# One hardware loop for the TensorE program of a decode attention kernel, with loads of 32 KB per partition

## The chip, the cores and the metric

The kernel runs on one core of one Trainium2 chip. The metric is the device time of one execution in microseconds (us), as the median of several executions. The profiled execution gives a "span", from its first to its last instruction, which is about 2 us shorter than its time.

PE is TensorE's matmul stream, PEld its weight loads, DVE VectorE, ACT ScalarE, SP the engine that issues the loads. All loads run on the core's 16 DMA engines. A "packet" is one record of one DMA engine: here one row of a load, or, as an "instruction packet", a piece of an engine's own program that is fetched. "Share" is the busy share of the 16 DMA engines together.

## The reference

Two decode attentions with one query position each, concatenated:

```python
# A: 32 heads, each with its own cache of 32768 keys;  Dh = 128, D = 512
q = (x @ wq).reshape(1, 1, 32, 128).transpose(0, 2, 1, 3)
scores = einsum("bhqd,bhkd->bhqk", q, k_cache) * 128 ** -0.5
o = einsum("bhqk,bhkd->bhqd", softmax(scores), v_cache)
a = o.transpose(0, 2, 1, 3).reshape(1, 1, 4096) @ wo
# B: the same with 32 query heads on 8 caches, and only the last 4096 keys of each
return concatenate([a, b], axis=-1)            # (1, 1, 1024), bf16
```

A's caches are 2 x 32 x 32768 x 128 bf16 numbers, 537 MB; everything together is 570 MB, and each byte is used once. In the kernel before, the load queue fills 98.5% of the 16 DMA engines' span (q1 below), so the least time is taken here as the time of the loads.

## The kernel before

Keys are loaded with a run of consecutive keys on each partition, transposed on PE in tiles of 128x128, copied from PSUM to SBUF by DVE, multiplied by the query (S), and the probabilities are transposed back (PT) and multiplied by V (PV). PE works in "rounds": 8 heads by 8192 keys for A. Helpers record every operation with what it depends on; the waits are then written out, so each engine's program is one straight line.

```python
a["KC"], b["KC"] = 4, 2            # A: a round is 2048*4 = 8192 keys by 32/4 = 8 heads
NK, NV, NT = 4, 3, 3               # 4 K slots of 2 MB, 3 V slots of 4 MB, 3 PSUM banks for transposes

def kv_src(self, name, which, h0, nh, r):      # one head: 64 keys = 16 KB per partition
    ap = d[which][0, h0:h0 + nh, base:base + d["blk"], :]
    return ap.rearrange("s (p j) d -> p s (j d)", p=128)

def emit_PV(self, i, u):           # 64 matmuls of 256 columns for 4 MB of V
    for kc in range(KC):
        for jj in range(4):
            for c in range(STRIPS):
                inst = e.matmul(acc[32*c:32*c+HG, 0:w], lhsT=pt[:, col:col+HG],
                                rhs=vv[:, :, 16*kc + 4*c + jj, :], ..., tile_position=(0, 32*c))
# ... end of the program: V of the last round, B's weights in between, A's weights last
for u in range(d["nvu"]):
    self.load_v(last, u, 0); self.load_v(last, u, 1)
    if u in (1, 2): self.load_wo("B", u - 1)
    if u == d["nvu"] - 1:
        for part in range(3): self.load_wo("A", part)
        self.emit_proj("B", ...)
    self.emit_PV(last, u)
self.emit_proj("A", ...)
```

## Time and profile before

| | before |
|---|---|
| time, median of 3 | 1368.06 us |
| span of the profiled run | 1365.0 us |
| first data packet, from the start | 2.06 us |
| last data packet | 1357.5 us, 7.6 us before the end |
| PE / DVE busy | 70% / 56% |
| instruction packets of PE | 119 of 16 KB |

The lines below are from the page of the kernel before. The strings of digits and the GB/s are 40 equal slices of the span; the queue lines give packets, MB and the share of 16 engines' span; then comes the chain of waits by engine, and the last line is the group of PE's transposes (busy us, mean ns of one, then idle time before them and what ended most of it).

```profile
span 1365.0 us, 32343 instructions
...
PE 951.6 (70%) x15172; PEld 734.7 (54%) x15172; DVE 767.8 (56%) x1414; ACT 29.9 (2%) x73; POOL 2.4 (0%) x11
...
DMA  9999999999999999999999999999999999999995
GB/s 392 422 425 426 427 426 427 427 425 427 425 426 427 426 426 427 425 426 427 427 424 427 425 427 427 425 426 426 427 426 425 426 426 428 426 426 425 426 405 213
...
q1 hardware_dynamic: 40340, 570.44, 98.5%
q8 instruction: 119, 1.95, 0.6%
...
DMA 77%; PE 20%; DVE 1%; issue 1%; SPq 0%; ACT 0%
...
L417 PE MATMUL psT<-ident,kbuf 128*128 128x128 bf16 x8448 | 641.3, 243 | 361.2 <-DMA kbuf<-in_A_k_cache_dram 294.9
```

DMA is busy in every slice but the last, it is 77% of the chain of waits, and PE's transposes idle 295 us for K. The rate stands at 426 GB/s for 36 slices. The end by stretches (columns: stretch, its length, busy us of each engine, PE clock, DMA share, GB/s):

```profile
...
600.00:1290.00 690.00, 485.77 (x7866) 379.57 (x7864) 395.20 (x699) 12.69 (x32) 0.00 (x0) 0.85 1.01 426
...
1300.00:1304.00 4.00, 3.70 (x97) 2.63 (x94) 2.77 (x6) 0.00 (x0) 0.00 (x0) 1.00 0.60 250
1304.00:1338.00 34.00, 11.87 (x203) 7.08 (x203) 6.58 (x28) 1.74 (x5) 0.00 (x0) 0.70 1.00 423
1340.00:1356.00 16.00, 9.59 (x96) 4.54 (x95) 2.26 (x6) 0.00 (x0) 0.00 (x0) 0.71 0.52 218
```

### The profile page before, as it was taken

The page shows a single profiled execution, that of the slowest core. Times are in us where ns is not written, and L with a number is a line of the kernel's source. Part 1 is how long each engine was busy: PE and PEld are TensorE (multiplying, and loading weights), DVE is VectorE, ACT ScalarE, POOL GpSimd, SP SyncE. Part 2 cuts the span into 40 slices and gives each one's busy share as a digit, 9 for nine tenths or more (in the row PEclk, how much of TensorE's full clock was granted, in tenths as well). Part 3 has the DMA queues.
Part 4 walks back from the last instruction along what each step waited for, and adds up shares of the span by engine and source line. Part 5 has one row for each costly group of instructions (what it writes and reads, how often), then busy time and mean ns, then how long its engine had stood idle before and what let it go on. Part 6 is the DMA issues. An engine that isn't in the chain of part 4 may idle for free.

```text
span 1365.0 us, 32343 instructions
## 1 busy us (share of the span) xinstructions
PE 951.6 (70%) x15172; PEld 734.7 (54%) x15172; DVE 767.8 (56%) x1414; ACT 29.9 (2%) x73; POOL 2.4 (0%) x11
## 2 busy tenths in 40 slices
PE   5689766776777687676667767766766767687646
PEld 4466555655555465555556545555655545465423
DVE  4688555655656555564655646555565656555431
ACT  0000000000000000000000000000000000000000
POOL 0000000000000000000000000000000000000000
PEclk9889878878988887887888888878888898887877
DMA  9999999999999999999999999999999999999995
GB/s 392 422 425 426 427 426 427 427 425 427 425 426 427 426 426 427 425 426 427 427 424 427 425 427 427 425 426 426 427 426 425 426 426 428 426 426 425 426 405 213
DMA packets 40762, 572.51 MB, mean 419 GB/s; under 512 B 4659, under 2 KB 4661, under 8 KB 4789
## 3 DMA queue, kind: packets, MB, share of 16 engines
q1 hardware_dynamic: 40340, 570.44, 98.5%
q8 instruction: 119, 1.95, 0.6%
q14 instruction: 15, 0.11, 0.0%
q10 hardware_dynamic: 288, 0.00, 0.0%
HBM read 570.43 MB, written 0.00 MB: 418 GB/s over the span
## 4 chain that ended last, share of the span: by engine, by line
DMA 77%; PE 20%; DVE 1%; issue 1%; SPq 0%; ACT 0%
DMA kbuf<-in_A_k_cache_dram 73%; PE psT L417 15%; PE psS L444 3%; DMA kbuf<-in_B_k_cache_dram 3%; DMA vbuf<-in_A_v_cache_dram 2%; PE psS L583 1%; PE psACC L525 1%; DVE kt L421 0%; SPq L203 0%; DVE oc_B L551 0%; PE psPT L565 0%; ACT psb L472 0%; DVE o_B L535 0%; DVE tr_in L460 0%; DVE nbg_B L491 0%
## 5 line engine op out<-in xcount | busy, mean ns | idle before, releaser
L421 DVE COPY kt<-psT 128x1024 bf16<-128x1024 bf16 x1056 | 672.5, 685 | 427.0 <-PE psT L417 423.7
L417 PE MATMUL psT<-ident,kbuf 128*128 128x128 bf16 x8448 | 641.3, 243 | 361.2 <-DMA kbuf<-in_A_k_cache_dram 294.9
L417 PEld LDWEIGHTS psT<-ident,kbuf 128*128 128x128 bf16 x8448 | 577.5, 111 | 489.8 <-DMA kbuf<-in_A_k_cache_dram 335.6
L444 PE MATMUL psS<-kt,qz_A 128*32 128x512 bf16 x2048 | 177.2, 427 | 0.0
L525 PE MATMUL psACC<-vbuf,ptsb 128*8 128x256 bf16 (+1 forms) x4160 | 132.9, 283 | 23.9 <-issue 21.7
L525 PEld LDWEIGHTS psACC<-vbuf,ptsb 128*8 128x8 bf16 (+1 forms) x4160 | 103.0, 89 | 55.2 <-issue 23.4
L537 DVE SCALAR_TENSOR_TENSOR o_A<-o_A,alpha_A,psACC 128x256 f32<-128x256 f32 x48 | 23.1, 480 | 87.5 <-PE psACC L525 87.5
L444 PEld LDWEIGHTS psS<-kt,qz_A 128*32 128x32 bf16 x2048 | 32.1, 97 | 31.5 <-issue 10.4
L472 ACT ACTIVATE psb<-psS,nb_A 128x512 bf16<-128x512 f32 x16 | 11.0, 687 | 1157.8 <-DVE nb_A L470 1157.8
L535 DVE COPY o_A<-psACC 128x256 f32<-128x256 f32 x16 | 6.8, 424 | 19.9 <-PE psACC L525 19.9
L503 PEld LDWEIGHTS psPT<-ident,psb 128*128 128x128 bf16 x72 | 5.7, 123 | 15.3 <-issue 11.8
L503 PE MATMUL psPT<-ident,psb 128*128 128x128 bf16 x72 | 10.2, 290 | 2.9 <-ACT psb L472 2.9
L460 DVE TENSOR_REDUCE tr_in<-psS 128x1 f32<-128x512 f32 x18 | 12.2, 680 | 0.0
L507 ACT ACTIVATE ptsb<-psPT 128x512 bf16<-128x512 bf16 x18 | 10.7, 596 | 52.8 <-PE psPT L503 52.8
L395 PE MATMUL psACC<-x_B,vbuf 128*128 128x1 bf16 x128 | 3.7, 165 | 11.5 <-DMA x_B<-in_B_x_dram 10.9
L551 DVE SCALAR_TENSOR_TENSOR oc_A<-o_A,gmask_A,oc_A 128x128 f32<-128x128 f32 x28 | 9.9, 352 | 1.0
L395 PEld LDWEIGHTS psACC<-x_B,vbuf 128*128 128x128 bf16 x128 | 3.6, 104 | 11.6 <-DMA x_B<-in_B_x_dram 10.9
L479 DVE SCALAR_TENSOR_TENSOR l_A<-l_A,alpha_A,rs_A 128x1 f32<-128x1 f32 x12 | 2.6, 220 | 12.3 <-ACT alpha_A L477 12.3
L588 DVE CAST out_sb<-psS 1x512 bf16<-1x512 f32 x2 | 1.4, 678 | 14.1 <-PE psS L583 14.1
L583 PE MATMUL psS<-kbuf,oz_A 128*1 128x512 bf16 x32 | 8.3, 422 | 0.6 <-DVE oz_A L572 0.6
L583 PE MATMUL psS<-kbuf,oz_B 128*1 128x512 bf16 x32 | 7.1, 379 | 0.0
L583 PEld LDWEIGHTS psS<-kbuf,oz_A 128*1 128x1 bf16 x32 | 2.8, 90 | 5.6 <-issue 2.4
(72 smaller groups left out, 83.4 us busy)
## 6 DMA issues: line engine op xcount, KB each, us to landing
kbuf<-in_A_k_cache_dram SPq DMA_DIRECT2D x128, 2048.0 KB, 33.8
vbuf<-in_A_v_cache_dram SPq DMA_DIRECT2D x128, 2048.0 KB, 38.4
kbuf<-in_B_k_cache_dram SPq DMA_DIRECT2D x4, 2048.0 KB, 28.8
vbuf<-in_B_v_cache_dram SPq DMA_DIRECT2D x4, 2048.0 KB, 37.4
vbuf<-in_B_wq_dram SPq DMA_DIRECT2D x2, 2048.0 KB, 9.8
vbuf<-in_A_wq_dram SPq DMA_DIRECT2D x2, 2048.0 KB, 28.6
kbuf<-in_B_wo_dram SPq DMA_DIRECT2D x2, 2048.0 KB, 36.9
kbuf<-in_A_wo_dram SPq DMA_DIRECT2D x1, 2048.0 KB, 38.8
```

What stands on the lines that cost most here:

```text
L395: inst = e.matmul(ps[:, h:h + 1], lhsT=wq[:, 4096 * tt + 128 * h:4096 * tt + 128 * h + 128], rhs=t["x"][:, tt:tt + 1], start=(tt == 0 and ...
L417: inst = e.transpose(T[:, 128 * k:128 * k + 128], self.kbuf[slot][:, DH * tile:DH * tile + DH], self.ident[:, :])
L421: self.tcopy.append(self.op("dve", lambda v, T=T, KT=KT: v.tensor_copy(KT[:, :], T[:, :]), o, self.sread.get(b - self.NKT)))
L444: inst = e.matmul(bank[32 * c:32 * c + 32, :], lhsT=t["qz"][:, off:off + 32], rhs=self.kt[(b0 + c // 2) % self.NKT][:, 512 * (c % 2):512 * ...
L460: o = dve(lambda v: v.reduce_max(tr["in"][:, 0:1], self.S[i % 2][:, :], axis=AXX), sdone)
L472: e = self.op("act", lambda s: s.activation(out=pb[:, :], in_=self.S[i % 2][:, :], func=ACTF.Exp, bias=t["nb"][:, r:r + 1], scale=self.SCA ...
L503: inst = e.transpose(PT[:, 128 * jj:128 * jj + 128], pb[:, 128 * jj:128 * jj + 128], self.ident[:, :])
L507: "act", lambda s: s.activation(out=pt[:, :], in_=PT[:, 0:512], func=ACTF.Copy), o, self.pvlast.get(i - 2))
L525: inst = e.matmul(acc[32 * c:32 * c + HG, 0:w], lhsT=pt[:, col:col + HG], rhs=vv[:, :, 16 * kc + 4 * c + jj, :], start=(kc == 0 and jj == ...
L537: ou = self.op("dve", lambda v: v.scalar_tensor_tensor(out=t["o"][:, osl], in0=t["o"][:, osl], scalar=t["alpha"][:, r:r + 1], in1=acc[:, 0:w],
L551: prev = self.op("dve", lambda v, src=src, gm=gm: v.scalar_tensor_tensor(out=t["oc"][:, :], in0=src, scalar=gm, in1=t["oc"][:, :], op0=ALU ...
L583: inst = e.matmul(bank[0:1, 0:512], lhsT=t["oz"][:, a:a + 1], rhs=self.wo_at(name, a), start=(a == 0), stop=(a == 31), skip_group_check=True)
```

## The change

The intent: PE's program for A becomes one hardware loop over 31 of its 32 rounds, so a round must look the same every time: same buffers, and waits that count tokens (a wait takes them off the semaphore) instead of waiting for an ever larger number. A round is now 2 heads by 16384 keys; each load is 4 MB with 32 KB per partition; there are 2 K slots and 2 V slots of 4 MB (16 MB, before 20 MB). S has one PSUM bank instead of two, the transposes have four instead of three. The softmax maximum is merged over the strips every round, and the output is accumulated already masked. The end of the program is ordered anew.

```diff
-        a["KC"], b["KC"] = 4, 2
+        a["KC"], a["HG"], b["KC"], b["HG"] = 8, 2, 2, 16
-        self.kbuf = [sb(f"kbuf{i}", [128, SLOT_TILES * DH], BF16) for i in range(self.NK)]
-        self.vbuf = [sb(f"vbuf{i}", [128, 2 * SLOT_TILES * DH], BF16) for i in range(self.NV)]
+        self.kbuf = [sb(f"kbuf{i}", [128, UT * DH], BF16) for i in range(2)]     # UT = 128 tiles
+        self.vbuf = [sb(f"vbuf{i}", [128, UT * DH], BF16) for i in range(2)]
 ...
+                for sem, n in o.take:
+                    e.sem_inc(sem, -n)._wait_ge(sem, n)
 ...
+                        with e.Fori(0, len(its)):
+                            for o in its[first]:
+                                emit_one(e, o, seen)
 ...
+            for u in range(2):                       # one round, two units (heads)
+                self.load_kv("k", name, g, r, u)
+                self.load_kv("v", *prev[u])
+                self.emit_unit(name, g, r, u, hooks)
+                self.emit_PV(*prev[u], ...)
+            self.emit_round_end(name, g, r)
 ...
+        for u in range(2):                           # the end
+            self.load_kv("v", name, g, r, u)
+        for n in ("B", "A"):
+            for part in range(len(self.WO_CUTS[n]) - 1):
+                self.load_wo(n, part)
 ...
+        for u in range(2):
+            self.emit_PV(name, g, r, u, pt=0, final=True)
+        self.emit_gather("A", a["NG"] - 1, a["NG"])
+        self.emit_spread("A")
+        self.emit_proj("B", self.S, 512)
+        self.emit_proj("A", self.PT, 0)
```

## The prediction

> **What bounds it now.** DMA. The DMA view gives the load queue 98.5% of the 16 engines' span; the slices hold 425-428 GB/s from 70 to 1290 us; PE is busy 70%, DVE 56%. The chain of waits is 77% DMA, and PE idles mostly for K loads. [...] The end is poor: the last two slices reach 405 and 213 GB/s; from 1303 us V loads wait for PV to free slots, and 7.5 us remain after the last data packet (output projection at 258 ns a matmul, cast, store). This tail costs about 18 us.
>
> **What the change does.**
> 1. Rows of 32 KB instead of 16 KB per partition for the large cache. Packet records show medians of 159, 312, 460 and 613 ns for 4, 8, 12 and 16 KB: about 302 ns per 8 KB plus 10 ns fixed. 32 KB should take 1216 ns against 2x613. Each engine moves about 2100 packets of 16 KB: I estimate 10.5 us saved, plus 1 us of completion packets (9 ns each). All on the critical path.
> 2. Tail: all V loads are queued before the output weights and V slots come free earlier, so the queue should stay full to the last 0.5 MB of weights; then 4 matmuls, cast, store. Estimate: 7 to 9 us saved.
> 3. Instruction fetch: 119 packets of 16 KB (0.6% of DMA) slow the data packets they overlap (1081 ns), raising the mean from 614 to 617 ns, some 5 us in all. The loop body, about 1200 instructions of 64 B, is 77 KB. Refetched every round, traffic rises slightly; resident, up to 5 us are saved. [...] I expect refetching.
> 4. PE/DVE: PV goes to twice as many matmuls of half the width. Now 64 take 1.92 us (30 ns each); one-column matmuls with their weight loads also run at 29 ns, so I expect 128 in about 3.7 us. Softmax statistics (3 us on DVE) come once per 16 MB and hold up the transpose copies. A round: 8 pairs of steps at 2.5 us (four 0.62 us copies) + 2x3.7 + 3 + 1 = 31 to 32 us[...]. DMA needs 39 us for a round's 16 MB. PE stays off the path.
> 5. Buffers: 16 MB instead of 20 MB, in 4 MB pieces. A K slot is needed again 29 us after it landed and is free after 11-14 us: no starving.
>
> **Sum.** 1368 - 11.5 - 8 - 1 = about 1347 us. Range 1337 to 1363. Chances: faster by over 2% 0.22, within 2% 0.66, slower 0.12.
>
> **What would show it.** 32 KB packets of about 1216 ns, slices near 430 GB/s (1); last slice well above 213 GB/s (2); instruction packets about 150 if refetched, below 40 if resident (3); PE busy up 8 points, PV near 30 ns a pair, PE still waiting on K every round (4); no dip in mid-run (5).
>
> **What would make it wrong.** Rows split into smaller packets (no gain in 1, about 1358); [...] PV far above 30 ns a pair, making PE the bound (slower); instructions resident plus a clean tail (just over 2% faster).

The sum: 1368 - 11.5 for the rows - 8 for the tail - 1, which the record does not assign, = 1347.5, written as about 1347.

## The result, and the profile after

The kernel after takes 1348.74 us (median of 4, 1348.43 to 1349.52), the kernel before 1367.96 us in the same rounds. A ratio here is the mean time of one kernel's fast runs over that of the other's fast runs of the same rounds, so not quite the ratio of the medians: it is 0.9857 (95% interval 0.9839 to 0.9875).

The page of the kernel after, the same lines as before:

```profile
span 1347.5 us, 42022 instructions
...
PE 929.0 (69%) x19316; PEld 770.9 (57%) x19316; DVE 803.5 (60%) x1664; ACT 57.6 (4%) x169; POOL 2.0 (0%) x14
...
DMA  9999999999999999999999999999999999999985
GB/s 400 422 429 428 431 433 429 433 432 432 429 433 432 433 430 430 434 432 430 432 432 431 431 433 432 431 430 433 432 433 428 434 432 430 430 435 431 431 337 254
...
q1 hardware_dynamic: 21412, 570.44, 98.6%
q8 instruction: 15, 0.25, 0.1%
...
L401 PE MATMUL psT<-ident,kbuf 128*128 128x128 bf16 x8448 | 630.9, 245 | 370.3 <-PEq L139 366.0
```

The plateau rose from 426 to 432 GB/s (rows16k below, which keeps the loop but has 16 KB rows, has 428), and the instruction packets of PE fell from 119 to 15. PE still waits 366 us in front of its transposes; the page puts this wait down to PE's sequencer because it is a token now. These are 63 waits, two a round, each in front of the first transposes of a unit (one head of the round), and the token that these take is the landing of K. The last two slices, 337 and 254 against 405 and 213, have not become better. By stretches, and the last pieces of the chain of waits (start us, us, what):

```profile
...
600.00:1290.00 690.00, 473.25 (x10147) 400.00 (x10148) 419.55 (x853) 29.86 (x90) 0.00 (x0) 0.84 1.00 432
...
1298.00:1304.00 6.00, 5.41 (x188) 4.05 (x185) 4.71 (x9) 0.00 (x0) 0.00 (x0) 1.00 0.15 49
1304.00:1334.00 30.00, 17.90 (x318) 11.54 (x319) 4.82 (x24) 1.56 (x4) 0.00 (x0) 0.72 0.98 413
1334.00:1338.00 4.00, 4.00 (x20) 1.51 (x18) 0.00 (x0) 0.00 (x0) 0.00 (x0) 0.99 0.13 54
```

```profile
...
1303.39 24.93 DMA kbuf<-in_B_wo_dram
1328.32 0.04 issue
1328.36 9.89 PE psS L569 x32
1338.26 6.92 PE psPT L569 x32
1345.18 0.02 issue
1345.20 0.68 DVE out_sb L573
```

The half-busy stretch is gone: 12 of the 16 engines end between 1333.7 and 1334.3 us, the last at 1337.6. There is a new hole of 6 us at 1298, where the last V load waits for PV and everything stands in line behind it. And both projections run at the very end, one after the other.

A packet's time by its size, from the packet records of both traces (medians):

| bytes | 4096 | 8192 | 12288 | 16384 | 32768 |
|---|---|---|---|---|---|
| before, ns | 159 | 312 | 460 | 613 | - |
| after, ns | 159 | 312 | 460 | 611 | 1216 |

**Following one engine.** The records name no DMA engine, but one engine's packets can be followed: each starts 3 to 4 ns before its predecessor on that engine ends, and every load ends on every engine with a packet of 4 bytes. Because of the overlap, what counts is the step from one start to the next: 610 ns for 16 KB and 1213 ns for 32 KB, so 7 ns of a packet do not grow with its size.

It also shows what an instruction packet does. It stands in the row of one DMA engine like any other packet, and the data packet after it is slowed as well. For PE's 16 KB that is 1.06 us plus 0.49 us, together 1.55 us (median of 109 of the 111 in mid-run of before); for 8 KB it is 0.32 plus 0.66, together 0.97 us. PE's packets go to eight of the engines in turn (in before, the engine was the same again eight packets later in 94 of the 100 cases compared). The 8 KB packets fall, 13 of 15 in after, on one engine that is not among those eight.

**A ledger of the slowest engine.** The kernel cannot end before its slowest DMA engine. If every packet of an engine took its median step, its work would take 1329.5 us before (2104 packets of 16 KB at 610 ns, and the smaller ones) and 1321.3 us after (1048 of 32 KB at 1213 ns). These two are worked out, and good to about 1 us because the steps are whole ns; the third row is what is left over; the others are read off.

| us | before | after | difference |
|---|---|---|---|
| first data packet | 2.06 | 1.95 | -0.1 |
| work of one engine at median steps | 1329.5 | 1321.3 | -8.2 |
| what the slowest engine lags behind that | 25.9 | 14.4 | -11.5 |
| from the last data packet to the end | 7.6 | 9.9 | +2.3 |
| span | 1365.0 | 1347.5 | -17.5 |

So two terms gained and one gave back. The experiments ask what the lag of the third row is, because nothing in the prediction names it, and whether the other rows are what they seem.

### The profile page after: what moved, and what is told of

The parts are those of the page before. It is cut to its first block, busy times and chain, and to the rows that moved or that the text cites. A ratio compares the mean times of both kernels' runs of the same rounds, so it can differ in the third digit from the quotient of the medians.

```text
span 1347.5 us, 42022 instructions
## 1 busy us (share of the span) xinstructions
PE 929.0 (69%) x19316; PEld 770.9 (57%) x19316; DVE 803.5 (60%) x1664; ACT 57.6 (4%) x169; POOL 2.0 (0%) x14
## 5 line engine op out<-in xcount | busy, mean ns | idle before, releaser
L401 PEld LDWEIGHTS psT<-ident,kbuf 128*128 128x128 bf16 x8448 | 589.2, 112 | 469.3 <-issue 468.1
L431 PE MATMUL psS<-kt,qw 128*32 128x512 bf16 x2048 | 165.3, 401 | 0.0
L499 PE MATMUL psACC<-vbuf,ptsb 128*2 128x128 bf16 (+1 forms) x8256 | 132.1, 222 | 17.5 <-issue 14.9
L499 PEld LDWEIGHTS psACC<-vbuf,ptsb 128*2 128x2 bf16 (+1 forms) x8256 | 122.3, 85 | 35.6 <-issue 20.4
L466 ACT ACTIVATE psb<-psS,nb_A 128x512 bf16<-128x512 f32 x32 | 22.0, 688 | 971.6 <-DVE nb_A L464 971.6
L528 DVE SCALAR_TENSOR_TENSOR oc_A<-psACC,hot_A,oc_A 128x128 f32<-128x128 f32 x48 | 16.9, 351 | 62.9 <-PE psACC L499 62.9
L431 PEld LDWEIGHTS psS<-kt,qw 128*32 128x32 bf16 x2048 | 33.0, 96 | 25.4 <-issue 4.3
L451 DVE TENSOR_REDUCE tr_in<-psS 128x1 f32<-128x512 f32 x34 | 23.5, 691 | 4.5 <-PE psS L431 2.1
L453 DVE COPY m<-tr_a 1x16 f32<-1x16 f32 (+1 forms) x136 | 22.3, 164 | 2.6
L460 DVE COPY b_A<-mr_A 1x16 f32<-1x16 f32 x128 | 21.1, 165 | 2.4
```

The costliest lines, as they stand in the source:

```text
L401: inst = e.transpose(T[:, 128 * k:128 * k + 128], src[:, DH * tile:DH * tile + DH], self.ident[:, :])
L431: inst = e.matmul(self.S[32 * c:32 * c + 32, :], lhsT=win, rhs=self.kt[(bb + c // 2) % NKT][:, 512 * (c % 2):512 * (c % 2) + 512], start=f ...
L451: o = dve(lambda v: v.reduce_max(tr["in"][:, 0:1], self.S[:, :], axis=AXX), sdone, self.k_pool)
L453: cps = [dve(lambda v, c=c: v.tensor_copy(m4[0:1, W * c:W * c + W], tr["a"][32 * c:32 * c + 1, 0:W]), o) for c in range(STRIPS)]
L460: x = dve(lambda v, c=c: v.tensor_copy(t["b"][32 * c:32 * c + 1, 0:W].rearrange("p (k h) -> p k h", k=KC), t["mr"][0:1, k, :].unsqueeze(1) ...
L466: self.op("act", lambda s: s.activation(out=self.psb[:, :], in_=self.S[:, :], func=ACTF.Exp, bias=t["nb"][:, k:k + 1], scale=self.SCALE, a ...
```

## The experiments

All twelve kernels gave correct results. Time is the median; the ratio is to the kernel before in the same rounds.

| label | base | time, us | ratio (95%) | last data packet, us |
|---|---|---|---|---|
| (before) | | 1366.9 to 1368.0 | 1 | 1357.5 |
| (after) | | 1348.74 | 0.9857 (0.9839-0.9875) | 1337.6 |
| unrolled | after | 1374.13 | 1.0055 (1.0039-1.0071) | 1359.0 |
| rows16k | after | 1358.97 | 0.9938 (0.9925-0.9950) | 1347.5 |
| tail_loads | after | 1352.26 | 0.9896 (0.9881-0.9910) | 1337.4 |
| tail_both | after | 1345.01 | 0.9836 (0.9823-0.9849) | 1337.5 |
| dve_pad | tail_both | 1360.04 | 0.9948 (0.9935-0.9962) | 1352.2 |
| wide_copy | tail_both | 1341.22 | 0.9811 (0.9798-0.9825) | 1333.6 |
| best | wide_copy | 1345.37 | 0.9839 (0.9826-0.9853) | 1333.6 |
| pv_wide | after | 1348.97 | 0.9866 (0.9851-0.9881) | 1337.5 |
| pv2 | after | 1489.86 | 1.0895 (1.0878-1.0911) | 1468.0 |
| pv3 | after | 1884.25 | 1.3797 (1.3776-1.3819) | 1852.2 |
| body93 | after | 1355.08 (one run) | - | 1339.5 |
| before_pv2 | before | 1377.95 | 1.0079 (1.0065-1.0093) | 1370.3 |

### unrolled: the loop undone, everything else kept

```diff
-                        if ops[k].loop is None:
+                        if True:                 # every round of PE is written out
```

> The kernel after with its hardware loop written out: same work, same tokens, but the PE program is fetched once from end to end, about 31 x 77 KB = 2.4 MB, so some 150 to 165 instruction packets instead of 15. Theory A (skew): fetches fall on about half of the 16 DMA engines and each costs its engine 1.2 to 1.5 us, so those engines end some 20 us late and the last one sets the time: 1361 to 1370 us, and the end of the run shows half the engines busy and half done. Theory B (mean, as in my prediction): the cost is the 5 us that the overlapped packets lose, spread over all engines: 1351 to 1354 us, engines ending together. Theory C: the loop itself costs PE time on the path: faster than after.

Measured: 1374.13 us, 25 us slower than after and slower than the kernel before. Theory B and C fall. From its trace, the instruction queue and two stretches of the end:

```profile
q8 instruction: 156, 2.56, 0.7%
```

```profile
...
600.00:1290.00 690.00, 492.54 (x10112) 396.17 (x10108) 408.63 (x858) 28.20 (x85) 0.00 (x0) 0.86 1.00 425
1302.00:1308.00 6.00, 3.62 (x109) 3.40 (x109) 0.35 (x1) 0.00 (x0) 0.00 (x0) 0.57 0.51 216
1320.00:1324.00 4.00, 1.20 (x87) 1.01 (x74) 0.17 (x1) 0.00 (x0) 0.00 (x0) 0.92 0.49 209
```

Here is the share of one half again, as in the kernel before: at 1302 us half of the engines have run dry and the other half have not. With 156 instruction packets this half lags; with 15 it does not. Spread over 8 engines, 156 packets are 19.5 for each, at 1.55 us a packet 30 us. In after the last engine is another one, that of the 8 KB packets, with 13 x 0.97 = 13 us. The difference, some 17 us, is most of the 21.4 us by which the last data packet moved in the profiled run. For the kernel before, 119 / 8 x 1.55 = 23 us, and the ledger shows a lag of 25.9.

The rest is not this lag, and a rival for it shows in the waits: first unrolled, then after (us in total, times, longest):

```profile
PE psACC L499 <- issue: 252.2, 63, 5.6
PE psT L401 <- PEq L139: 42.7, 33, 7.3
```

```profile
PE psT L401 <- PEq L139: 366.0, 63, 8.0
PE psACC L499 <- issue: 14.9, 4, 4.3
```

In unrolled PE waits 252 us at its PV for nothing the profile shows, which is probably its own program, and its wait for K has shrunk from 366 to 43 us: it has little slack left. The loads also stall in mid-run now, which neither before nor after shows: the DMA share falls to about 0.6 for 2 us near 688 and 809 us. The size was above what I expected (1361 to 1370); these stalls, by PE or by buffers that no longer bridge the lag, are a likely part of it, but no run separates them. So the 25 us are not all skew.

### rows16k: the loop kept, 16 KB rows

```diff
-        self.load(dst, src, sem[slot], free[slot])
+        for h in range(2):      # two loads of 16 KB rows; B split by heads, wq likewise; PE takes 32 tokens
+            self.load(dst[:, :, 8192*h:8192*h+8192], src[:, :, 8192*h:8192*h+8192], sem[slot], free[slot])
```

> The kernel after, loop kept, with each 4 MB load issued as two loads of 16 KB rows. If the fixed cost of a packet is what the 32 KB rows saved: 16 KB packets of 613 ns, 1360 us (11 to 12 us above after). If row size does not matter: 1349 us, within 2 us of after. If the two smaller loads help by landing K sooner: below 1348.

Measured: 1358.97 us, 10.2 us above after; the median of a 16 KB packet was 614 ns, and the last data packet came 9.9 us later. The row size is worth about what the prediction said. The ledger's median steps give about 8 us of this; the rest is more lag of the slowest engine (16 us by the same sum, after 14). That term of the prediction is shown.

### tail_loads and tail_both: filling the hole at the end

```diff
 # tail_loads
-        for u in range(2):
-            self.load_kv("v", name, g, r, u)
-        for n in ("B", "A"): ...load_wo
+        self.load_kv("v", name, g, r, 0)
+        self.load_wo("B", 0)
+        self.load_kv("v", name, g, r, 1)
+        for part in range(3):
+            self.load_wo("A", part)
 # tail_both: also, on PE, B's projection ahead of the last PV
+        self.emit_PV(name, g, r, 0, pt=0, final=True)
+        self.emit_proj("B", self.S, 512)
+        self.emit_PV(name, g, r, 1, pt=0, final=True)
```

> The kernel after with B's output weights (4 MB) loaded ahead of the last V load, order of PE kept. Theory: the hole in the DMA between 1297 and 1304 us (6 to 7 us lost), because the last V load must wait for PV and everything stands in line behind it, is filled, data end near 1330 us instead of 1337.6. But PE still does both projections after the last PV, 17 us one after the other, so only 3 to 5 us are gained: 1344 to 1346. Rival: the DMA alone bounds the end, then 1341 to 1342.

> As tail_loads, with B's projection also moved ahead of the last PV on PE. Theory: the 10 us of B's projection now run while the last V and A's weights come in, so both the hole (6 to 7 us) and the serial projection (about 5 us) are saved: 1335 to 1340 us, DMA data ending near 1330 us. If the hole was not what held the end, within 2 us of tail_loads.

Measured: tail_loads 1352.26 us, slower than after, and tail_both 1345.01 us. Both expectations missed, and in an instructive way: the hole was filled (DMA share 0.97 or more from 1290 to 1324 us), yet the last data packet came at 1337.4 and 1337.5 us, just as in after at 1337.6. So the hole had cost nothing on the path. Two stretches of tail_both show why:

```profile
...
1304.00:1324.00 20.00, 14.50 (x188) 9.37 (x189) 3.41 (x18) 1.56 (x4) 0.00 (x0) 0.74 0.98 419
1328.00:1337.00 9.00, 6.57 (x145) 3.38 (x146) 1.03 (x4) 0.00 (x0) 0.00 (x0) 0.81 0.07 28
```

For the last 9 us the share is 0.07, one engine of sixteen. Followed engine by engine, 15 had their last data between 1324.2 and 1328.0 us and one at 1337.5. A single engine is 10 us behind all others; it never ran dry in the hole, so filling the hole for the fifteen others changed nothing. tail_loads was slower because the last V, which this engine delivers late, now stood behind B's weights (PV began at 1328 us), with both projections still to come: 12.2 us from the last data packet to the end. tail_both gained over after because that stretch shrank from 9.9 to 6.6 us. This is the row of the ledger that gave back: B's projection in line with A's.

### dve_pad and wide_copy: what holds up that one engine

The packet records of after show one packet of 1875 ns instead of 1216 about every 100 us, each at the time of an 8 KB instruction packet on queue 14. DVE runs about 124 instructions in 100 us (1664 in 1347 us), 8 KB at 64 bytes each (as in before, where 1.95 MB were fetched for 30344 PE instructions), so these looked like DVE's program.

```diff
 # dve_pad, on tail_both
                 self.emit_PV(*prev[u], ...)
+                for n in range(50*i + 25*u, 50*i + 25*u + 25):
+                    self.op("dve", lambda v, n=n: v.memset(self.pad[0:1, n:n+1], 0.0))
 # wide_copy, on tail_both: 16 transposes into two PSUM banks, one copy of both
-        self.T = [ps(f"psT{i}", [128, 512], F32) for i in range(4)]     # copies of 128x1024 bf16, 1056 times
+        self.T = [ps(f"psT{i}", [128, 1024], F32) for i in range(2)]    # copies of 128x2048 bf16, 528 times
-            for k in range(8):
+            for k in range(16):
```

> tail_both plus 1600 memsets of one element on DVE (25 after each PV), which nobody waits for: about 100 KB more DVE program. Theory A (skew): the programs of the other engines are fetched in 8 KB pieces, each holds up one packet of one DMA engine by 0.66 us (1875 against 1216 ns), always on the same engine; some 12 more pieces put this engine 8 us further behind, and the run ends with it: 1351 to 1355 us against 1345, the last data packet at about 1345 instead of 1337.5. Rival: what lags is that engine for another reason and DVE's program is harmless; DVE's 100 us more of busy time hide in its waits: within 2 us of tail_both.

> tail_both with the transposed K copied out two PSUM banks at a time: 528 copies of 2048 columns instead of 1056 of 1024, so 34 KB less DVE program. Theory A (skew): about 4 pieces fewer, the lagging engine 2 to 3 us earlier, the last data packet near 1335: 1342 to 1343 us. Rival: no change (within 1 us), or slower because the coarser copies lengthen each round on PE and DVE past what DMA needs.

Measured: 1360.04 and 1341.22 us. The instruction queue of the other engines, first tail_both, then dve_pad, then wide_copy:

```profile
q14 instruction: 15, 0.12, 0.0%
```

```profile
q14 instruction: 29, 0.23, 0.0%
```

```profile
q14 instruction: 11, 0.09, 0.0%
```

| | DVE instructions | q14 packets | last data packet, us |
|---|---|---|---|
| wide_copy | 1136 | 11 | 1333.6 |
| tail_both | 1664 | 15 | 1337.5 |
| dve_pad | 3264 | 29 | 1352.2 |

Four packets fewer came with 3.9 us, which is 4 x 0.97. The queue line of dve_pad counts one packet of 96 bytes, so 13 pieces of 8 KB more came with 14.7 us: 12.6 us at 0.97, the rest not explained. My 0.66 us was too small, because it left out that the slowed packet has first waited 0.32 us for the instruction packet; hence 1360 and not 1351 to 1355. And in dve_pad a single engine was again the last, at a share of 0.07 for 12 us:

```profile
...
1304.00:1338.00 34.00, 27.71 (x489) 20.69 (x490) 15.04 (x62) 1.56 (x4) 0.00 (x0) 0.85 0.97 409
1340.00:1352.00 12.00, 7.07 (x148) 3.50 (x148) 1.71 (x5) 0.00 (x0) 0.00 (x0) 0.86 0.07 30
```

The rival, that DVE's program is harmless, falls. Memsets that nobody waits for cost 15 us, while DVE stayed below 62% busy. The 25 memsets after a PV took DVE 0.36 us, and its busy time rose from 804 to 823 us in all, not by the 100 us that the expectation feared. wide_copy is the fastest kernel.

### best: one more step at the end, which failed

```diff
-        self.load_wo("B", 0)                        # 4 MB ahead of the last V
+        self.load_wo("B", 0)                        # 2 MB ahead, 2 MB behind; the projection split likewise
         self.load_kv("v", name, g, r, 1)
+        self.load_wo("B", 1)
```

> wide_copy with B's output weights in two halves, one before and one after the last V load, and B's projection split the same way. The last V lands 5 us sooner, so A's projection can start when its weights land rather than after them: 1338.5 to 1341 us against 1341.2. Rival: the cold PE (309 ns a matmul) leaves the end where it was, within 1 us.

Measured: 1345.37 us, slower than wide_copy by 4 us, so the name turned out wrong. The last data packet was at 1333.6 us in both. The rival's 309 ns are wide_copy's last projection: 32 matmuls in 9.89 us, the first of them one every 0.43 us, the last 17 one every 0.21 us, with a granted clock of 0.50 from 1328 to 1333 us; "cold" is only a name for that. In the last PV of its profiled run PE stood still:

```profile
1319.68 1.78 PE L501 MATMUL psACC<-vbuf,ptsb 128*2 128x128 bf16 x113 [1.03 <-PEq L139]
...
1325.85 0.59 PE L501 MATMUL psACC<-vbuf,ptsb 128*2 128x128 bf16 x15 [4.39 <-issue]
```

The wait is put down to "issue", which means nothing the profile shows; an instruction packet started at 1323 us in that trace, so PE probably waited for the program of its tail, behind the loads. The two profiled runs are no fair pair: that of best was its fastest (1344.61 us), that of wide_copy its slowest (1343.78 us), so their spans, 1342.9 and 1342.1 us, lie closer than the medians. They also ran on different chips, but each against the kernel before in the same rounds (0.9839 and 0.9811). The explanation is only argued.

### pv_wide, pv2, pv3, body93: is PE off the path, and how much program stays

```diff
 # pv2 (pv3: 3; body93: 2 for the first unit of a round only)
-            for kc in range(KC):
+            for kc in [k for _ in range(2) for k in range(KC)]:      # the second time overwrites
 # pv_wide: 256 columns in place of 128; the other tile goes to PSUM columns nobody reads
+            T, x0, x1 = (T, 128, 384) if T % 2 == 0 else (T - 1, 0, 256)
+            rhs = vv[:, 0, T:T + 2, :]
```

> The kernel after with every PV product computed twice (the second overwrites the first, result unchanged): 2 us more PE work per unit, 4 us per round, loop body 110 KB. If PE is off the path with some 8 us of slack a round: within 2 us of after (1349). If PE were near the bound: plus 60 us or more. Instruction packets stay near 17 if 110 KB still stays resident; about 240 and 15 us or more slower if not.

> As pv2 but three times: 8 us more PE work a round (about 31 + 8 = 39 us against DMA's 39), loop body about 143 KB. [...] the body no longer fits: some 280 instruction packets, half the DMA engines 40 us behind, well over 1380 us. If it still fits: some 19 packets, and at most 20 us over after, from PE alone.

> The kernel after with every PV matmul of the large cache streaming 256 columns instead of 128 (the second tile goes to PSUM columns nobody reads; result unchanged). As much extra array time as in pv2 (about 2 us a unit, 4 us a round), but the loop body stays at 77 KB. If pv2 was slow because its 110 KB body is fetched again every round: within 2 us of after (1349), 15 instruction packets. If PE has no slack of 4 us a round: about 1470 as in pv2.

> The kernel after with the PV of the first unit of a round computed twice, body about 93 KB, to find where residency ends (77 KB stays, 110 KB does not). If a 93 KB body stays: 15 to 17 instruction packets and about 1350 us. If not: over 80 packets and above 1370 us. I lean to staying (0.6).

Measured: pv2 took 1489.86 us, 141 us more than after. Taken alone this would have said that PE has no room at all, against all I had argued. pv_wide, with about as much more array time and the body unchanged, took 1348.97 us, the same as after: its PV of one unit lasts 3.67 us (1.96 in after, 3.75 in pv2). So PE is off the path by at least 3.4 us a round, and what hurt pv2 is the size of its body. First pv_wide (instruction queue and one PV), then pv2 (instruction queue and two of its largest waits; us in total, times, longest):

```profile
q8 instruction: 15, 0.25, 0.1%
...
613.40 3.67 PE L505 MATMUL psACC<-vbuf,ptsb 128*2 128x256 bf16 x128
```

```profile
q8 instruction: 155, 2.54, 0.7%
```

```profile
PEld psACC L499 <- issue: 218.6, 79, 5.8
PE psACC L499 <- issue: 204.0, 67, 5.6
```

In after the same PV waits for issue 15 us in all. pv2 fetches 140 packets more than after, 4.5 a round, and PE, which runs 16 KB of PV program in about 2 us, waits for them up to 5.8 us at a time. pv3 fetches 324 packets and takes 1884 us. body93 fetched 18 packets, none of them between 176 and 1321 us, so a 93 KB body stays; it took 1355.08 us in its one run, and 13.5 us of that are from the last data packet to the end (9.9 in after), where four of its 18 packets fall. After itself fetches no PE instructions between 136 and 1312 us. The limit lies between 93 and 110 KB (counted as 64 bytes an instruction: 1.95 MB for the 30344 PE instructions of the kernel before).

### before_pv2: the same theory in the kernel before

```diff
 # on the kernel before
-            for kc in range(KC):
+            for kc in [k for _ in range(2) for k in range(KC)]:
```

> The kernel before with every PV product computed twice (result unchanged): 4160 more matmuls and weight loads, 0.53 MB more PE program, some 33 more instruction packets (119 to 152), all of it work that PE has room for (PE waits for K in every unit). Theory A (skew): 33 more fetches on half the DMA engines put these 4 to 6 us further behind (18 us now for 119), and they set the end: 1371 to 1374 us. Theory B (mean): about 1.3 us more: 1368 to 1369.5. If PE is starved by the fetches, as in pv2, far more, and the PE's idle time would be put down to issue.

Measured: 1377.95 us, 11 us more with 152 instruction packets instead of 119. This is the right side of the rival, which said 1.3 us, but not clean. The slices of its start are 392, 422, 357, 416 GB/s: some 4.5 us of DMA time were lost between 90 and 98 us, where B gives way to A, and the extra PE work can do that without any skew between the engines. About 6 us are left for the skew, which fits 33 packets / 8 x 1.55 = 6.4 us. I count it as in agreement, not as proof.

## Why the prediction was right or wrong

The time was predicted as 1347 us and measured as 1348.74, inside the range and the class. Two of the terms behind it were wrong, and their errors cancelled: that the sum came within 2 us is luck.

1. **Rows of 32 KB: right, slightly over-sized.** Predicted 11.5 us; undoing it on the chip cost 10.2, and the ledger has 8.2. A 32 KB packet took 1216 ns, the number predicted, but 3 to 4 of the 10 ns that I called fixed overlap the next packet. The plateau rose to 432 GB/s (430 predicted). It was measured with one core running; what sets it is not shown.
2. **The tail: wrong.** "the queue should stay full to the last 0.5 MB of weights; then 4 matmuls, cast, store. Estimate: 7 to 9 us saved." The queue ran dry at 1298 us (share 0.15), because the last V load waits for a PV and all the weights stand behind it. B's projection then waited for its weights and took 9.89 us, A's 6.92 us behind it: 9.9 us instead of 7.6 from the last data packet to the end. The term was +2.3 us. Also my reading of the tail of before was wrong: its 16 us at a share of 0.52 were not a queue run low by V slots, but eight engines finished by 1345 us and eight behind until 1357.
3. **Instruction fetch: the term was mis-sized, and its sign too.** "I expect refetching", and at most "some 5 us in all". The 77 KB body was not fetched again (15 packets), and the lag of the slowest engine fell from 25.9 to 14.4 us. It did not fall further because the next slowest engine, that of DVE's program, was then the last. Against the same kernel unrolled the loop is worth 25 us, of which some 17 are this lag (worked out, above). The step that failed is the division by 16: I spread the delay of the overlapped packets over all engines, and left out the time of the instruction packet itself. Fetches fall on few engines, a packet costs its engine 1.55 us (16 KB, PE) or 0.97 us (8 KB), and the kernel ends with the slowest.
4. **PE off the path: right, its costs over-sized.** PV took 1.96 us for 128 matmuls, 15 ns each, not 29; PE's busy share went from 70% to 69%, not up by 8 points. I had taken the pace of the query projection, which loads 128 columns of weights each time; PV loads 2. A transpose of as many columns, with 128 columns of weights, took 61 ns (32 in 1.96 us), four times 15; why PV is so much faster no run separates. Statistics took 3.1 us (3 predicted). A stall of PE at the loop's branch was not shown by any run: at the head of each round PE waits for K anyway (5.8 us at 597 us and 5.3 us at 637 us in after), and a stall under that wait would not be seen.
5. **Buffers: right for this kernel.** No slice of the plateau dips (428 to 435 GB/s from the third slice to the 38th). unrolled shows dips near 688 and 809 us; whether the 16 MB are too little under a larger lag or PE was late is not separated.

What stays open: why PE's fetches go to eight engines in turn and DVE's to one; why the packet after a fetch is slowed; how the rest of the 25 us of unrolled divides; and what makes best slower than wide_copy in its timed runs.

## What to carry to other kernels

When a kernel is bound by its loads, look at the slowest DMA engine and not at the mean: a DMA share that stands at one half, or at one sixteenth, at the end of the run can mean that some engines are behind (0.52 in before with eight behind, 0.07 in tail_both with one); the packet records followed engine by engine tell. Then filling holes for the others need not help: here it left the last data packet at 1337.4 and 1337.5 us, after 1337.6. Program size was DMA traffic that fell unevenly in these runs (PE's packets on eight engines at 1.55 us each, 13 of DVE's 15 on one more at 0.97 us), so a hardware loop (25 us against unrolled) or fewer, larger instructions (3.8 us, wide_copy against tail_both) can gain time on engines that are not the bound themselves, as long as the loop's body stays resident (93 KB did here, 110 KB did not, and that cost 141 us). To test whether an engine is off the path, lengthen its instructions and do not add to them (pv_wide took 1348.97 us, pv2 with about as much more PE work 1489.86).
